# Weight loads in fewer, larger transfers behind one key tile, and query tails turned back behind them

## The chip, the core and the metric

The kernel runs on one core of a Trainium2 chip. The metric is device time in microseconds (us), lower is better. Engines are named as in the profile: PE (matrix products), PEld (its weight loads), DVE (vector), ACT (scalar and activation functions), POOL (GpSimd), SP (sync, which here only issues transfers).

## What is computed

For x of 2048 tokens by 640 features, all in bfloat16, with a token's gate g:

```python
g = sigmoid((x * gate_w).sum(-1, keepdims=True))

# a: linear attention, 32 heads of 20
q, k, v = split(x @ wqkv)
pq, pk = phi(q), phi(k)            # phi(t) = (t + 1 if t > 0 else exp(t)) + 1e-6
kv  = einsum("shd,she->hde", pk, v);  z = pk.sum(over tokens)
a   = (pq @ kv) / (pq . z + 1e-6) @ wo

# b: a mixer block and an MLP
h   = gelu(layernorm(x) @ w1)      # 640 -> 640
hs  = four groups of 160 features of h, shifted by +1, -1, +2, -2 tokens, @ w2
x1  = x + hs
b   = x1 + gelu(layernorm(x1) @ w3) @ w4     # 640 -> 1728 -> 640

out = g * a + (1 - g) * b
```

## The kernel before

Everything stays in SBUF. Tokens are cut into 16 tiles of 128 and 4 chunks of 512, features into 5 blocks of 128. "Turning" a tile means a transposing transfer, issued by SP, which puts features on the partitions.

**First stage, to 52.8 us on PE.** For each token tile PE makes 512 columns of q (`q_tile`, L900) and the keys (`k_tile`, L798); ACT's Exp and two DVE instructions make phi of them (`phi`, L788). The last 128 columns of q are made for a whole chunk at once, already turned (`q_turned`, L888); the result `mT` has to be turned back into token order by a transfer on SP (`q_back`, L896). There are four such tails. The turned x (`xT`) comes from transfers on SP (`x_turn`, L689). An event `k_done[t]` marks the last DVE instruction of key tile t.

**Second stage, 52.8 to 76 us.** PE forms GT, the product of x and phi(k) over all tokens (`gt_step`, L827); one block of it is copied by ACT to Mt and turned by SP into GT (L825). From GT and `wv` follow the heads' kv (`kvt_group`, L993), and from these and `wo` the matrix M (`m_last`, `m_first`, L1047 and L1052), stored in `M_sb`. Within this stage the layer norm of x is prepared: POOL computes the statistics of a chunk (`ln_chunk_stats`, L840) and normalises a tile into one of three `xn` slots (`normalize`, L865), SP turns it into `xnT` (`t_xn`, L871).

**Then** come w1 (`w1_group`, L1090, one block j of output features for one chunk), w2 (`w2_tile`, L1098), w3 and w4 with M's product mixed in, and the output.

**The mixer's feature order.** w1's 640 columns are used as four groups of 160, each with a shift of its own. Blocks j = 0 to 3 are the first 128 columns of each group, block 4 the four remainders of 32. Before, this order is made by the transfers: w1 is loaded by 8 transfers (128 and 32 columns of each group), w2 by 8 (128 and 32 rows of each).

**What sets the order.** Each piece of work is an item in one of several streams with dependences and a model of time (`_Items.run`, L336): among the items whose dependences have been emitted, a planner takes the one that can begin soonest, and so writes out a fixed instruction list for each engine. `sch.dma(queue, ...)` (L260) issues a transfer from the named engine's queue; `deps` are events that the issuing engine waits for. Each engine runs its list strictly in order, so a waiting instruction holds all behind it. The weights w1, w2, wv and wo are loaded from POOL's queue by `load_w1`, `load_w2` and `load_wvo` (L722 to L749), behind key tiles 7, 9 and 11. SP's list in this stretch is: turns of x, three query tails, GT, turns of xn. The items that place these are L955 to L979.

Of the kernel before, what the change touches and what calls it, by code (L numbers as in the profile page):

```python
# [5 lines left out]
BF16 = mybir.dt.bfloat16  # L6
# [5 lines left out]
D = 640  # L12
# [3 lines left out]
NT = S // 128  # L16
NCH = S // 512
KD = D // 128
# [398 lines left out]
def _build(nc, A_x, A_wqkv, A_wo, B_w1, B_w2, B_w3, B_w4, gate_w, out, dbg=None, stop=None):  # L417
    sch = _Sched(nc)
# [37 lines left out]
    pa = Arena(SB_LO, SB_HI - SHARED)  # L456
# [3 lines left out]
    ps = nc.alloc_psum_tensor("ps", [128, 8, 512], F32)  # L460
# [14 lines left out]
    w1 = pa.alloc("w1", [128, KD, D], BF16)  # L475
    w2 = pa.alloc("w2", [128, KD, D], BF16)
    wo_aug = pa.alloc("wo_aug", [128, 6, D], BF16)
    x_tok = pa.alloc("x_tok", [128, NT, D], BF16)
    xnT = pa.alloc("xnT", [128, KD, S], BF16)
# [3 lines left out]
    Lt = pa.alloc("Lt", [128, 6, 64], BF16)  # L483
    Mt = pa.alloc("Mt", [128, D], BF16)
    M_sb = pa.alloc("M_sb", [128, KD, D], BF16)
    zb = pa.alloc("zb", [128, D], BF16)
    dnr = pa.alloc("dnr", [128, 2, 4, H], F32)
    zc = pa.alloc("zc", [128, KD], F32)
# [13 lines left out]
    wv = wvf[:, 0:KD * D].rearrange("p (k d) -> p k d", d=D)  # L502
# [58 lines left out]
    def nfree(ap):  # L561
        n = 1
        for d_ in ap.shape[1:]:
            n *= d_
        return n
# [23 lines left out]
    def pe(fn, reads, writes, cost=500.0):  # L589
        for w_ in writes:  # L590
            sp_, rl = sch.rects(w_)
            if sp_ == "ps":
                for (_p0, _p1, lo, hi) in rl:
                    for b in range(lo // PS_BANK, (hi - 1) // PS_BANK + 1):
                        bank_pend.discard(b)
        return sch.op("pe", fn, reads, writes, cost=cost)

    def mm_group(out_ap, pairs, reads_extra=()):
        n = len(pairs)

        def fn(e, out_ap=out_ap, pairs=pairs, n=n):
            ins = None
            for i, (l, r) in enumerate(pairs):
                ins = e.matmul(out_ap, l, r, start=(i == 0), stop=(i == n - 1))  # L604
            return ins
        reads = [a for p in pairs for a in p] + list(reads_extra)
        return pe(fn, reads, [out_ap], cost=n * (max(nfree(pairs[0][1]), 24) * 0.4167 + 2.5))
# [54 lines left out]
    def memset(engf, ap, val):  # L662
        return engf(lambda e: e.memset(ap, val), [], [ap])

    def copy(engf, out_ap, in_ap):
        cost = None
        if engf is dve and in_ap.dtype == BF16 and out_ap.dtype == BF16:
            cost = 65.0 + nfree(out_ap) / 1.92
        return engf(lambda e: e.tensor_copy(out_ap, in_ap), [in_ap], [out_ap], cost=cost)
# [50 lines left out]
    k_done = {}  # L720

    def load_w1():  # L722
        dp = [k_done[7]]
        for g_ in range(4):
            sch.dma("pool", w1[:, :, 128 * g_:128 * (g_ + 1)],
                    B_w1[:, 160 * g_:160 * g_ + 128].rearrange("(k p) f -> p k f", p=128), "w1", group_total=8, deps=dp)
            sch.dma("pool", w1[:, :, 512 + 32 * g_:512 + 32 * (g_ + 1)],
                    B_w1[:, 160 * g_ + 128:160 * (g_ + 1)].rearrange("(k p) f -> p k f", p=128), "w1", group_total=8, deps=dp)

    def load_w2():  # L730
        dp = [k_done[9]]
        for g_ in range(4):
            sch.dma("pool", w2[:, g_, :], B_w2[160 * g_:160 * g_ + 128, :], "w2", group_total=8, deps=dp)
            sch.dma("pool", w2[32 * g_:32 * (g_ + 1), 4, :], B_w2[160 * g_ + 128:160 * (g_ + 1), :], "w2", group_total=8, deps=dp)

    def wo_rows(h, e, ns):
        v = A_wo[0:600, :].rearrange("(q p) d -> p q d", p=B3)
        q0 = 2 * h + e
        return v[:, q0:q0 + 4 * (ns - 1) + 1:4, :]

    def load_wvo():
        dp = [k_done[11]]
        sch.dma("pool", wv[:, :, :], A_wqkv[:, 2 * D:3 * D].rearrange("(k p) f -> p k f", p=128), "wv", deps=dp)
        for h in range(2):
            for e in range(2):
                ns = 3 - h
                sch.dma("pool", wo_aug[64 * h:64 * h + B3, e:e + 2 * ns - 1:2, :],
                        wo_rows(h, e, ns), "wo", group_total=5, deps=dp)
        sch.dma("pool", wo_aug[64:104, 4, :], A_wo[600:D, :], "wo", group_total=5, deps=dp)  # L749

    memset(pool, ones_c[:], 1.0)
    memset(pool, wkg[:, :, D:D + 1], 1.0)
# [20 lines left out]
    IT = _Items()  # L773
# [24 lines left out]
    def k_tile(t):  # L798
        tok = slice(128 * t, 128 * (t + 1))
        b = pair()  # L800
        mm_group(ps[:, b, 0:512], [(xT[:, k, tok], wkg[:, k, 0:512]) for k in range(KD)])
        mm_group(ps[:, b + 1, 0:130], [(xT[:, k, tok], wkg[:, k, 512:D + 2]) for k in range(KD)])
        k_out(t, b)
# [61 lines left out]
    def normalize(which, t, st):  # L865
        sx = slot("xn", 3)
        tag_set("xn", sx, (which, t))
        xn_slots[(which, t)] = sx
        ts(pool, xn[:, sx, :], x_tok[:, t, :], st[:, 6, t:t + 1], st[:, 7, t:t + 1], ALU.mult, ALU.add)
# [18 lines left out]
    def q_turned(c):  # L888
        b = bank()
        sl = qx_slot[c] = slot("tl", 4)  # L890
        mm_group(ps[:, b, :], [(wq[:, k, 512:D], xT[:, k, 512 * c:512 * (c + 1)]) for k in range(KD)])
        phi(b, mT[:, sl, :], n=512)
# [3 lines left out]
    def q_back(c):  # L896
        sl = qx_slot[c]
        sch.dma("sp", pq_tok[:, 4 * c + 1:4 * c + 5, 512:D], mT[:, sl, :], "trm%d" % sl, transpose=True)

    def q_tile(t):  # L900
        tok = slice(128 * t, 128 * (t + 1))
        b = bank()
        mm_group(ps[:, b, :], [(xT[:, k, tok], wq[:, k, 0:512]) for k in range(KD)])
        phi(b, pq_tok[:, t + 1, 0:512], n=512)
# [36 lines left out]
    def addA(name, dur, fn, deps=()):  # L941
        IT.add("A", name, dur, fn, deps)
# [7 lines left out]
    for i in range(3, NT + 2):  # L950
        if i < NT:
            addA(("q", i), 1.08, lambda t=i: q_tile(t))
            addA(("k", i), 1.36, lambda t=i: k_tile(t))
            if i % 4 == 3:
                addA(("qx", i // 4), 1.08, lambda c=i // 4: q_turned(c))  # L955
                IT.add("QB", ("qb", i // 4), 0.0, lambda c=i // 4: q_back(c),
                       deps=[(("qx", i // 4), 2.5), (("t1", NT - 1), 0.0) if i == NT - 1 else (("k", i + 1), 0.0)])
        if i > 3:
            for t in range(3) if i == 4 else (i - 2,):
                addA(("g0", t), 0.27, lambda t=t: gt_tail(t), deps=[(("k", max(t, 1)), 2.0)])  # L960

    IT.add("LW", ("lw1",), 0.0, load_w1, deps=[(("k", 7), 0.0)])
    IT.add("LW", ("lw2",), 0.0, load_w2, deps=[(("k", 9), 0.0)])
    IT.add("LW", ("lwv",), 0.0, load_wvo, deps=[(("k", 11), 0.0)])

    def stats1(c):
        ln_chunk_stats(st1, c, lr[:, 4 * c:4 * c + 4, 0:1].rearrange("p t o -> p (t o)"))

    for u in range(NT):
        if u % 4 == 0:  # L970
            IT.add("S1", ("s1", u // 4), 0.0, lambda u=u: stats1(u // 4), deps=[(("k", u + 3), 1.8)])
        d1 = [(("s1", u // 4), 3.0 + 0.9 * (u % 4))]
        d1.append((("k", 13), 0.0) if u == 0 else (("n1", u - 1), 0.9))
        if u == 2:
            d1.append((("k", NT - 1), 2.0))
        if u >= 3:
            d1.append((("t1", u - 3), 0.0))
        IT.add("N1", ("n1", u), 0.0, lambda u=u: normalize(1, u, st1), deps=d1)
        IT.add("T1", ("t1", u), 0.0, lambda u=u: t_xn(1, u), deps=[(("n1", u), 1.1)] + ([(("zb",), 0.0)] if u == 12 else []))  # L979
# [110 lines left out]
    def w1_group(c, j):  # L1090
        cols = slice(512 * c, 512 * (c + 1))
        b = bank()
        mm_group(ps[:, b, :], [(w1[:, k, 128 * j:128 * (j + 1)], xnT[:, k, cols]) for k in range(KD)])
        for (p0, p1, sh) in PIECES[j]:
            o0 = 2 + 512 * c + sh
            activation(hsT[p0:p1, j, o0:o0 + 512], ps[p0:p1, b, :], ACTF.Gelu_apprx_tanh)
# [209 lines left out]
    for c in range(NCH):  # L1306
        for j in range(KD):
            deps = [(("t1", u), 0.9) for u in range(4 * c, 4 * c + 4)] if j == 0 else []
# [7 lines left out]
    for t in range(NT):  # L1316
        c = t // 4
        deps = [(("w1", c, KD - 1), GEL)]
# [8 lines left out]
    for u in range(NT):  # L1327
        deps = [(("s2", u // 4), 3.2 + 0.9 * (u % 4))]
# [8 lines left out]
    for c in range(NCH):  # L1337
        for j in range(KFF):
            deps = []
# [4 lines left out]
            if j == 0:  # L1344
                deps = deps0 + [(("t2", u), 0.9) for u in range(4 * c, 4 * c + 4)]
# [12 lines left out]
    for t in range(NT):  # L1358
        deps = [(("zb",), 1.0), (("q", max(t, 2)), 2.0), (("sg", 1), 0.0)]
        deps.append((("qb", t // 4), 3.0))  # L1360
        if t < 5:
            i = 4 * t + 3
            deps.append((("w1", i // KD, i % KD), 0.0))
        else:
            i = 3 * (t - 5)
# [7 lines left out]
    for t in range(NT):  # L1373
        g = GOF[t]
        t0, t1 = GROUPS[g]
        cl = (t1 - 1) // 4
        deps = [(("qt", t), 3.0), (("w4load",), 0.0), (("m", 1), 1.0), (("mt",), 2.5)]
# [65 lines left out]
```

## Time and profile before

| | |
|---|---|
| median of 3 runs | 259.44 us (259.2 to 259.5) |
| the profiled execution | 259.2 us |
| its span, first to last instruction | 257.9 us |
| PE busy | 255.1 us, 1478 matmuls |
| mean granted PE clock | 1.000 |
| POOL busy | 90.9 us |
| software queue (POOL's transfers) | 1168 packets, 3.28 MB |
| hardware queue of SP | 54800 packets, 21.87 MB |

A row of a group or a timeline names the line of the code, the engine, the operation, and "written<-read". In a timeline the first number is the start in us from the span's start, the second the length; x16 means that sixteen neighbouring instructions are put together, and the brackets at the end say how long the engine sat idle before and which work ended that. For transfers the table of issues gives the size and the median time from issue to landing; an issue's own length is the time of the issuing engine, not of the data. The chain of work that ended last is the path that sets the end.

### The profile page before, as it was taken

What the parts mean: (1) busy time and instruction counts of PE and PEld (TensorE: products, weight loads), DVE (VectorE), ACT (ScalarE), POOL (GpSimd) and SP (SyncE); (2) the same over time, 40 slices, a digit from 0 to 9 for tenths busy, and PEclk for the clock granted to TensorE, in tenths of its full rate; (3) what the DMA queues carried; (4) which work ended last, traced back from release to release, by engine and by line L of the source; (5) the groups of instructions that cost most, each with busy time, mean ns of one, the idle gap of its engine ahead of it and who ended that gap; (6) DMA issues with size and microseconds to landing.
All of it is one profiled execution on the core that took longest, in us unless ns stands there. A gap on an engine that the chain in (4) does not pass through costs nothing.

```text
span 257.9 us, 3904 instructions
## 1 busy us (share of the span) xinstructions
PE 255.1 (99%) x1478; PEld 126.7 (49%) x1478; DVE 144.8 (56%) x289; ACT 108.9 (42%) x224; POOL 90.9 (35%) x144
## 2 busy tenths in 40 slices
PE   8999999999999999999999999999999999999996
PEld 4555555544454545555444445444444744444744
DVE  2697888899964995589999300399700033200033
ACT  1587676651366868666854331001540100253100
POOL 5020499976952162677908000123200021300000
PEclk9999999999999999999999999999999999999999
DMA  7856699956637699372628630114130022200012
GB/s 226 226 135 114 188 137 177 262 109 126 127 76 79 125 399 293 84 100 56 121 49 117 123 60 3 31 25 127 36 17 0 3 52 80 102 1 3 0 20 102
DMA packets 57650, 26.50 MB, mean 103 GB/s; under 512 B 48884, under 2 KB 56221, under 8 KB 57632
## 3 DMA queue, kind: packets, MB, share of 16 engines
q1 hardware_dynamic: 54800, 21.87, 40.2%
q0 software_dynamic: 1168, 3.28, 5.8%
q10 hardware_dynamic: 1664, 1.11, 1.4%
q8 instruction: 11, 0.18, 0.3%
q14 instruction: 7, 0.06, 0.1%
HBM read 12.04 MB, written 2.62 MB: 57 GB/s over the span
## 4 chain that ended last, share of the span: by engine, by line
PE 99%; DVE 0%; issue 0%
PE ps L604 53%; PE ps L1213 30%; PE ps L811 8%; PE ps L922 2%; PE ps L884 1%; PE ps L1240 1%; PE ps L1128 1%; PE ps L615 1%; PE ps L1009 0%; PE ps L1038 0%; PE ps L923 0%; DVE x_tok L643 0%
## 5 line engine op out<-in xcount | busy, mean ns | idle before, releaser
L604 PE MATMUL ps<-xnT,w 128*128 128x512 bf16 x360 | 81.3, 379 | 0.0
L643 DVE SCALAR_TENSOR_TENSOR x_tok<-ps,stg,abx 128x512 bf16<-128x512 f32 (+2 forms) x17 | 12.2, 718 | 81.4 <-PE ps L1213 81.3
L660 ACT ACTIVATE h2T<-ps 128x512 bf16<-128x512 f32 x52 | 30.6, 598 | 59.5 <-PE ps L604 59.5
L604 PEld LDWEIGHTS ps<-xnT,w 128*128 128x128 bf16 x360 | 34.5, 98 | 39.8 <-issue 0.5
L1213 PE MATMUL ps<-w,h2T 128*128 128x512 bf16 (+2 forms) x221 | 45.4, 366 | 0.0
L626 POOL TENSOR_SCALAR xn<-x_tok,st 128x640 bf16<-128x640 bf16 x32 | 36.0, 1130 | 25.4 <-DMA xnT<-xn 24.9
L626 POOL TENSOR_SCALAR abx<-x_tok,stg 128x640 f32<-128x640 bf16 x16 | 15.3, 965 | 70.7 <-DVE x_tok L643 70.7
L1213 PEld LDWEIGHTS ps<-w,h2T 128*128 128x128 bf16 x221 | 21.2, 98 | 23.5
L660 ACT ACTIVATE Er<-ps 128x512 bf16<-128x512 f32 (+1 forms) x36 | 23.0, 649 | 14.6 <-PE ps L604 10.3
L659 ACT ACTIVATE junk<-x_tok 128x640 bf16<-128x640 bf16 x32 | 23.6, 738 | 3.9 <-DVE x_tok L641 3.7
L660 ACT ACTIVATE hsT<-ps 128x512 bf16<-128x512 f32 (+1 forms) x32 | 19.0, 594 | 12.5 <-PE ps L604 12.0
L604 PE MATMUL ps<-w,hsT 128*128 128x512 bf16 (+1 forms) x160 | 23.7, 299 | 0.0
L604 PE MATMUL ps<-wkg,xT 128*128 128x130 bf16 (+1 forms) x140 | 21.4, 299 | 0.0
L641 DVE SCALAR_TENSOR_TENSOR x_tok<-ps,x_tok 128x640 bf16<-128x640 f32 x16 | 13.1, 821 | 11.2 <-PE ps L604 10.5
L604 PEld LDWEIGHTS ps<-w,hsT 128*128 128x128 bf16 x160 | 13.3, 98 | 12.3
L1213 PE MATMUL ps<-M_sb,pqnT 128*128 128x512 bf16 (+2 forms) x85 | 18.6, 367 | 0.0
L811 PE MATMUL ps<-pk_tok,x_tok 128*128 128x512 bf16 x80 | 17.8, 379 | 0.0
L604 PEld LDWEIGHTS ps<-wkg,xT 128*128 128x128 bf16 x140 | 11.9, 97 | 11.4
L1157 DVE TENSOR_TENSOR pq_tok<-pq_tok,dnr 128x300 bf16<-128x300 bf16 (+1 forms) x48 | 16.9, 405 | 0.5
L634 DVE TENSOR_TENSOR qprod<-qprod,pk_tok 128x640 f32<-128x640 f32 x13 | 16.3, 1252 | 0.4
L626 DVE TENSOR_SCALAR Er<-Er 128x512 bf16<-128x512 bf16 (+1 forms) x36 | 12.3, 341 | 6.9 <-ACT Er L660 6.2
L604 PE MATMUL ps<-wq,xT 128*128 128x512 bf16 x65 | 16.2, 379 | 0.0
(87 smaller groups left out, 243.8 us busy)
## 6 DMA issues: line engine op xcount, KB each, us to landing
w<-in_B_w_dram SPq DMA_DIRECT2D x1, 2160.0 KB, 8.1
w<-in_B_w_dram SPq DMA_DIRECT2D x1, 2080.0 KB, 15.2
out_dram<-x_tok SPq DMA_DIRECT2D x3, 640.0 KB, 3.2
w<-in_B_w_dram POOLq DMA_DIRECT2D x8, 160.0 KB, 6.4
x_tok<-in_A_x_dram SPq DMA_DIRECT2D x6, 160.0 KB, 3.7
x_tok<-in_A_x_dram SPq DMA_DIRECT2D x1, 960.0 KB, 5.3
wv<-in_A_wqkv_dram POOLq DMA_DIRECT2D x1, 800.0 KB, 5.7
x_tok<-in_A_x_dram SPq DMA_DIRECT2D x1, 640.0 KB, 4.6
```

What stands on the lines that cost most here:

```text
L604: ins = e.matmul(out_ap, l, r, start=(i == 0), stop=(i == n - 1))
L615: ins = e.transpose(o, s_, ident[:])
L626: return engf(lambda e: e.tensor_scalar(out_ap, in_ap, s1, s2, op0, op1), rd, [out_ap], cost=cost)
L634: return engf(lambda e: e.tensor_tensor(out_ap, a, b_, op), [a, b_], [out_ap], cost=cost)
L641: return dve(lambda e: e.scalar_tensor_tensor(out_ap, in0, scalar, in1, op0, op1, accum_out=accum), rd, [out_ap, accum], cost=cost + 70.0)
L643: return dve(lambda e: e.scalar_tensor_tensor(out_ap, in0, scalar, in1, op0, op1), rd, [out_ap], cost=cost)
L659: return act(lambda e: e.activation(out_ap, in_ap, func, bias=bias, scale=scale, accum_out=accum), rd, wr, cost=cost)
L660: return act(lambda e: e.activation(out_ap, in_ap, func, bias=bias, scale=scale), rd, wr, cost=cost)
L811: ins = e.matmul(o, l, r, start=(t0 + q_ == 0), stop=(t0 + q_ == NT - 1))
L922: ins = e.matmul(ps[:, b, 0:512], l, w[:, k, 0:512], start=(k == 0), stop=(k == KD - 1))
L1157: dve(lambda e, o=o, i0=i0, i1=i1: e.tensor_tensor(o, i0, i1, ALU.mult), [i0, dnr[:, 1, sd, :]], [o], cost=cost)
L1213: ins = e.matmul(o, l, r, start=first and i == 0, stop=last and i == len(prs) - 1, skip_group_check=True)
```

## The change

- w1 is loaded as it lies in memory, by one transfer instead of eight. Blocks 0 to 3 are read from it at a stride of 160 columns; the four remainders are put together by a copy on POOL into a new buffer `w1r`, which lies where M's first block will be stored later.
- w2 is loaded by five transfers instead of eight: the four groups' first 128 rows in one.
- All of w1, w2, wo and wv are issued behind key tile 8, in this order. Before, wv went ahead of wo.
- The first three query tails are turned back behind key tiles 14, 15 and 15 instead of 4, 8 and 12.
- The normalisation of tile 1 is placed behind the last piece of GT's tail block.

```diff
     M_sb = pa.alloc("M_sb", [128, KD, D], BF16)
+    w1r = pa.alias("w1r", [128, KD, 128], BF16, pa.last_addr, KD * D * 2)
...
     def load_w1():
-        dp = [k_done[7]]
+        sch.dma("pool", w1[:, :, :], B_w1.rearrange("(k p) f -> p k f", p=128), "w1", deps=[k_done[8]])
+
+    def w1_rest():
+        copy(pool, w1r[:, :, :].rearrange("p k (g f) -> p k g f", g=4),
+             w1[:, :, :].rearrange("p k (g f) -> p k g f", g=4)[:, :, :, 128:160])
+
+    def load_w2():
+        dp = [k_done[8]]
+        rows = B_w2.rearrange("(g r) d -> r g d", r=160)
+        sch.dma("pool", w2[:, 0:4, :], rows[0:128, :, :], "w2", group_total=5, deps=dp)
         for g_ in range(4):
-            sch.dma("pool", w1[:, :, 128 * g_:128 * (g_ + 1)],
-                    B_w1[:, 160 * g_:160 * g_ + 128].rearrange("(k p) f -> p k f", p=128), "w1", group_total=8, deps=dp)
-            sch.dma("pool", w1[:, :, 512 + 32 * g_:512 + 32 * (g_ + 1)],
-                    B_w1[:, 160 * g_ + 128:160 * (g_ + 1)].rearrange("(k p) f -> p k f", p=128), "w1", group_total=8, deps=dp)
-
-    def load_w2():
-        dp = [k_done[9]]
-        for g_ in range(4):
-            sch.dma("pool", w2[:, g_, :], B_w2[160 * g_:160 * g_ + 128, :], "w2", group_total=8, deps=dp)
-            sch.dma("pool", w2[32 * g_:32 * (g_ + 1), 4, :], B_w2[160 * g_ + 128:160 * (g_ + 1), :], "w2", group_total=8, deps=dp)
+            sch.dma("pool", w2[32 * g_:32 * (g_ + 1), 4, :], B_w2[160 * g_ + 128:160 * (g_ + 1), :], "w2", group_total=5, deps=dp)
...
     def load_wvo():
-        dp = [k_done[11]]
-        sch.dma("pool", wv[:, :, :], A_wqkv[:, 2 * D:3 * D].rearrange("(k p) f -> p k f", p=128), "wv", deps=dp)
+        dp = [k_done[8]]
...
         sch.dma("pool", wo_aug[64:104, 4, :], A_wo[600:D, :], "wo", group_total=5, deps=dp)
+        sch.dma("pool", wv[:, :, :], A_wqkv[:, 2 * D:3 * D].rearrange("(k p) f -> p k f", p=128), "wv", deps=dp)
...
                 IT.add("QB", ("qb", i // 4), 0.0, lambda c=i // 4: q_back(c),
-                       deps=[(("qx", i // 4), 2.5), (("t1", NT - 1), 0.0) if i == NT - 1 else (("k", i + 1), 0.0)])
+                       deps=[(("qx", i // 4), 2.5), (("t1", NT - 1), 0.0) if i == NT - 1 else (("k", min(14 + i // 4, NT - 1)), 0.0)])
...
-    IT.add("LW", ("lw1",), 0.0, load_w1, deps=[(("k", 7), 0.0)])
-    IT.add("LW", ("lw2",), 0.0, load_w2, deps=[(("k", 9), 0.0)])
-    IT.add("LW", ("lwv",), 0.0, load_wvo, deps=[(("k", 11), 0.0)])
+    IT.add("LW", ("lw1",), 0.0, load_w1, deps=[(("k", 8), 0.0)])
+    IT.add("LW", ("lw2",), 0.0, load_w2, deps=[(("k", 8), 0.0)])
+    IT.add("LW", ("lwv",), 0.0, load_wvo, deps=[(("k", 8), 0.0)])
+    IT.add("LW", ("w1r",), 0.0, w1_rest, deps=[(("k", 10), 0.0)])
...
+        if u == 1:
+            d1.append((("g0", NT - 1), 0.0))
...
-        mm_group(ps[:, b, :], [(w1[:, k, 128 * j:128 * (j + 1)], xnT[:, k, cols]) for k in range(KD)])
+        mm_group(ps[:, b, :], [(w1[:, k, 160 * j:160 * j + 128] if j < 4 else w1r[:, k, :], xnT[:, k, cols]) for k in range(KD)])
```

## The prediction

> **What bounds the kernel now.** I read the busy shares and the clock row first, then PE's busy time by stage, then the chain of work that ended last, and only then the queues that the change touches (POOL, SP and the table of DMA issues).
>
> ```profile
> PE 255.1 (99%) x1478; PEld 126.7 (49%) x1478; DVE 144.8 (56%) x289; ACT 108.9 (42%) x224; POOL 90.9 (35%) x144
> PEclk9999999999999999999999999999999999999999
> ```
>
> The clock is at its top digit in all 40 slices (mean 1.000), so none is to be won there. Since a matmul's end is modelled, 99% alone proves nothing. The table by stage has, after the stretch and its length, PE's busy us, then PEld, DVE, ACT and POOL:
>
> ```profile
> 9.40:52.80 43.40, 43.40 (x270) 22.51 (x269) 35.66 (x67) 31.46 (x80) 23.65 (x45) 1.00 0.86 168
> 52.80:69.80 17.00, 17.00 (x83) 7.81 (x81) 16.44 (x18) 5.53 (x10) 13.96 (x16) 1.00 0.57 113
> 69.80:256.00 186.20, 186.12 (x1086) 92.22 (x1083) 89.28 (x195) 69.28 (x132) 49.96 (x67) 1.00 0.37 79
> ```
>
> From 9.4 us to the end PE is idle for 0.08 us. That it isn't padded is seen by the chain (start, length, what):
>
> ```profile
> 46.58 2.44 PE ps L604 x15
> ...
> 49.29 3.52 PE ps L604 x20
> 52.81 17.00 PE ps L811 x81
> 69.82 4.32 PE ps L604 x20
> ```
>
> Twenty matmuls of 512 columns take 4.32 us, 0.216 each. The 81 of GT are 78 of 512 columns and 3 of 128; a pair of one each takes 0.27 in the chain, so 128 columns cost 0.055: 78 x 0.216 + 3 x 0.055 = 17.01, and 17.00 is measured. There is no hidden wait at the two places where the change could remove one: before 69.82, when the first w1 group needs turned rows 0 to 3, w1 and its weights, and in the k and q stage before it. **PE is the bound and has nothing to wait less for.**
>
> **What the change does to PE, ACT and DVE.** Laid side by side, their instruction streams in both programs are the same, in the same order and with the same waits by engine; only the four w1 groups of the fifth block read `w1r` instead of a tail of `w1`. No matmul is added or taken away: 0 us. The left operand lies elsewhere in SBUF; a weight load takes 98 ns beside a matmul of 216, so it could double and stay hidden. What remains is whether POOL, SP and the DMA queues make PE wait.
>
> ```profile
> 31.93 11.41 POOL L285 DMA_DIRECT2D w<-in_B_w_dram  x16
> 46.28 0.95 POOL L285 DMA_DIRECT2D wv<-in_A_wqkv_dram  x1
> 47.24 3.29 POOL L285 DMA_DIRECT2D wo_aug<-in_A_wo_dram  x5
> 50.58 0.88 POOL L626 TENSOR_SCALAR xn<-x_tok,st 128x640 bf16<-128x640 bf16 x1
> 29.07 8.30 SPq L281 DMA_TRANSPOSE xT<-x_tok  x6
> 37.41 6.68 SPq L281 DMA_TRANSPOSE pq_tok<-mT  x3
> 56.77 1.20 SPq L281 DMA_TRANSPOSE GT<-Mt  x1
> 58.02 13.46 SPq L281 DMA_TRANSPOSE xnT<-xn  x10
> ```
>
> **POOL.** Now: 11.41 + 0.95 + 3.29 = 15.65 us of issuing, 31.93 to 50.58 with one chunk of statistics (43.38 to 46.28, 2.90 us) between. After: the start moves from key tile 7 to key tile 8, whose last DVE instruction ends at 33.93. Then w1 in one transfer (0.95, the row of wv, which has the same shape), w2's 128 rows in one (from 0.87, the usual step between w1's issues now, to 0.95), four of 32 rows (the second half of the 16 takes 4.29 us for 8, so 0.54 each, 2.15), wo 3.29, wv 0.95: 8.3 us, to 42.2. The copy into `w1r` is not in the trace: at the low end it goes as the small POOL rows (0.30 for 128x60), at the high end twice the slowest pass over 128x640 (1.78), 3.6; I take the median row of such a pass, 0.93, as it has the same size. It waits for w1, and behind it on POOL stand the statistics of chunk 2, the normalisation of tile 0 and all later ones. w1 lands at the soonest 5.7 us after its issue (wv's row), so 39.6; at the latest when all 3.28 MB of the software queue are through. These at 209 GB/s (the mean from 50 to 56 us, nearly all loads) take 15.7 us, from about 36, so 51.7. By the first, statistics run from 43.1 to 46.0 and tile 0 is normalised at 46.9 instead of 51.46; by the second the copy ends at 52.6 and tile 0 is done at 56.4. **Neither reaches PE:** the first w1 group is at 69.82, and tiles 1 to 3 follow the statistics of chunk 3, which ACT holds back to 52.63 now anyway.
>
> **SP.** The turning of tile 0 moves ahead of three turned query tails and of GT: it goes out at about 47 instead of 58.02. The tails go from 37.41 to about 48, 1.3 us each (the row without back-pressure), done issuing by 52; GT waits for ACT's Mt until 56.74 as now. Tiles 1, 2 and 3 now go out at 59.34, 60.66 and 61.98 and land 2.7 later; with one turn less ahead each goes 0 to 1.3 earlier. Now tile 3 is in at 64.7, so the first group has 5.1 us of slack, afterwards 5.1 to 6.4. Tile 7 (67.43 + 2.7 = 70.1, needed at 77.36) has 7.2. If loads and tails delay all of it by the worst landing of any xnT turn (8.0 instead of 2.7), 5.3 is gone and 0.2 would be left to pay. The tails themselves are first read by DVE at 82.8; from 52 they have 30 us.
>
> **The other side of the transfers.** The loads that used to trickle out over 11.4 us now stand in the queues within 8.3 us, beside turns of x that the q and k tiles read.
>
> ```profile
> wv<-in_A_wqkv_dram POOLq DMA_DIRECT2D x1, 800.0 KB, 5.7
> w<-in_B_w_dram POOLq DMA_DIRECT2D x8, 160.0 KB, 6.4
> pq_tok<-mT SPq DMA_TRANSPOSE x4, 7.6
> ```
>
> The turns of x tiles 10 to 15 go out at 29.07, 30.31, 31.63, 32.95, 34.2 and 36.1; the first lands in 2.6, the last two in 7.1 and 7.2 us, because the loads run beside them. So tile 14 is in at 41.3, needed at 46.58, and tile 15 at 43.3, needed at 49.29: slack 5.3 and 6.0. Afterwards the loads start 2 us later, which spares tiles 12 and 13, and 14 and 15 meet a fuller queue. At best each lands in 2.6; at worst no turn moves until all loads are through at 51.7, tile 14 comes at 53.0 and PE pays 6.4. I take the row nearest to it, turns beside loads, 7 to 9 us (8.9 is the slowest tail): 36.1 + 8.9 = 45.0, in time. Cost 0, with 6.4 kept for the range.
>
> The packets counted over the queues are 2.8 KB on the software queue (3.28 MB in 1168) and 0.4 KB on the turning one. The Trainium skill, "DMA: Bandwidth & Descriptors", section "Queues, rings and completion order", speaks against the change here: an engine takes turns between queues by whole packets, so larger load packets make each turn wait longer; this case's 2.6 against 7.2 agrees in direction, no row shows larger packets. By it the sum would gain a stall of 0 to about 3 us; by the landings of this trace it gains none.
>
> DVE's pass over Er (128x640) takes 0.33 us at 28.64 and 40.58, but 0.64 at 32.44, when POOL starts issuing. A k tile needs DVE for 0.33 + 0.82 + 0.29 + 0.69 = 2.13 of PE's 2.71 us, so 0.3 more still fits. The bound is 0 to 0.3 on each of about four tiles, 1.2 in all; there were four such slow passes before at no PE idle time, so I take 0. The Trainium skill, "SBUF — State Buffer", section "SBUF: two separate sides", holds that POOL's descriptor writing and such DVE passes lock each other out; by it POOL's 8.3 us would stretch, into slack.
>
> **The sum.** 0 + 0 + 0 against the profiled execution's own 259.2 (span 257.9 and 1.3 around it). The median of the three runs is 259.44, 0.24 above it; a run like those gives **259.4**.
>
> **The rivals.**
> - **The burst holds up the turning of x, and it is slower.** Place: queries 14 and 15 at 46.58 and 49.29. It decides once a turn lands more than 12.4 us after issue for tile 14 or 13.2 for tile 15. For it: landings already go from 2.6 to 7.2, and the burst is denser. Against it: 5 us of slack. Price 0 to 6.4, middle 3: 262.4. Chance 0.08.
> - **POOL's new wait holds the first w1 group.** After the copy come 2.9 (statistics), 0.9, 3.9 (chunk 3), three tiles of 1.47 and 3.0 for issue and landing, 15.1 in all, so it decides when the copy ends after 54.7, w1 landing 20 us after issue where wv took 5.7. Price, at 2 us past that: 261.4. Chance 0.03.
> - **DVE is slowed past its slack** while POOL issues: tenths on some tiles, 260.2. Chance 0.04.
> - **The change doesn't do what it says:** the larger transfers land no sooner. All are needed late (w1 69.82, w2 80.6, wv 76.29, wo 92.9), so 259.4 as well. Chance 0.10.
> - **Faster.** Only the first 9.4 us hold idle time or slow spots, and nothing there is changed; a chance difference of some tenths, 258.7. Chance 0.05.
>
> **How the numbers follow.** The forecast, loads earlier and PE unmoved, has 0.70. A measurement of this kernel tells 0.2%, 0.52 us, from no change: 258.9 to 259.9 is "same", with 0.70 + 0.10 = 0.80; slower has 0.08 + 0.03 + 0.04 = 0.15, faster 0.05. The range reaches from 258.9 over the DVE case and the small end of the first rival to 260.5; what lies above (large stalls, 0.09) and below (0.05) is left out.
>
> **What would show it.** Right: PE's chain without gaps, its span within 0.5 us of 257.9; POOL done issuing near 42, not 50.6; tile 0 turned near 47; the three tails after it. Wrong: an idle entry of PE behind a DMA on xT (k and q stage) or xnT (69.82), the turns of tiles 14 and 15 landing in over 12 us, or the copy into `w1r` after 54.

## The result, and the profile after

The changed kernel takes **269.37 us** (median of 6 runs, 265.74 to 271.02) against 259.47 (6 runs, 259.20 to 260.23): ratio 1.0306, 95% interval 1.0250 to 1.0363. It is slower by 3%; the prediction said no change, 258.9 to 260.5. The profiled execution took 270.29, its span is 269.0. The ratio is over the three runs that lie within 1.5% of the fastest (265.74, 268.34, 268.47); the other three count as slow and the profiled one is among them, so the pieces below add up to 11.1 us where the ratio stands for some 8.

Busy shares and the clock row of the changed kernel's page:

```profile
PE 257.3 (96%) x1478; PEld 127.1 (47%) x1478; DVE 143.3 (53%) x289; ACT 108.9 (40%) x224; POOL 85.1 (32%) x135
PEclk9999999858999999999999999999999999999999
```

PE's work is the same 1478 matmuls. What is new is a dip of the clock in slices 8 to 10 (6.7 us each, so some 47 to 67 us), where it was 9 everywhere, and a PE share of 96% instead of 99%. The list of what PE waited for (total us, times, longest):

```profile
PE ps L605 <- DMA xT<-x_tok: 8.3, 1, 8.3
PE ps L885 <- PEq L1432: 0.8, 1, 0.8
PE ps L923 <- DMA wq<-in_A_wqkv_dram: 0.5, 2, 0.4
```

The first line is new: one wait of 8.3 us for a turn of x. The 0.8 stands in every profile of this kernel, the 0.5 on the first loads comes and goes (0.4 to 1.1 in four of the experiments, with nothing changed there). The chain of waits between 44 and 82 us (start, length, what):

```profile
36.40 21.54 DMA xT<-x_tok
57.94 0.05 issue
57.99 5.88 PE ps L605 x20
63.87 17.00 PE ps L812 x81
```

The turn of x tile 15 goes out at 36.40 and lands at 57.94. Then the 20 matmuls of that tile (query, key, turned queries) take 5.88 us where they took 3.52, and GT's 81 take 17.00, as before, but begin at 63.87 instead of 52.81. So 11.06 us are lost up to here: 8.3 of waiting, 5.88 - 3.52 = 2.36 of slow matmuls, and about 0.4 already before the wait (PE comes to it at 49.7, where query 15 began at 49.29 before). Span against span is 269.0 - 257.9 = 11.1, so nothing is lost after it. The clock, by stretches (the last three columns are granted clock, DMA share and GB/s):

```profile
46.00:50.00 4.00, 3.70 (x26) 1.89 (x24) 3.58 (x6) 2.51 (x7) 0.73 (x1) 1.00 1.01 136
50.00:54.00 4.00, 0.00 (x0) 0.00 (x0) 1.15 (x2) 0.95 (x4) 0.00 (x0) 0.78 1.29 201
54.00:58.00 4.00, 0.01 (x1) 0.02 (x2) 0.00 (x0) 0.00 (x0) 0.00 (x0) 0.50 0.81 125
58.00:62.00 4.00, 4.00 (x10) 1.48 (x11) 0.98 (x2) 0.60 (x1) 0.00 (x0) 0.50 0.40 80
62.00:64.00 2.00, 2.00 (x15) 1.06 (x13) 0.40 (x2) 1.17 (x3) 0.27 (x1) 0.88 0.00 0
64.00:66.00 2.00, 2.00 (x13) 0.94 (x12) 1.89 (x5) 0.83 (x4) 1.37 (x4) 1.00 0.03 8
```

PE stops at 49.7; the clock is at half all the way from 54 until 62, four us after PE has work again at 57.99, and full from 64. The 0.78 from 50 to 54 is 1.76 us at 0.50 and the rest at 1.00, so it fell near 52.2, some 2.5 us after PE stopped. Ten matmuls fit into 58 to 62, at 0.216 us it would be 18.

Now the landings. In a window of some hundredths of a us around one issue, the issue table holds that issue alone (last number: us from issue to landing). Tiles 14 and 15 in the changed kernel, then the same two in the kernel before:

```profile
xT<-x_tok SPq DMA_TRANSPOSE x1, 10.2
xT<-x_tok SPq DMA_TRANSPOSE x1, 21.5
```

```profile
xT<-x_tok SPq DMA_TRANSPOSE x1, 7.1
xT<-x_tok SPq DMA_TRANSPOSE x1, 7.2
```

Tile 14 (issued 35.08) lands at 45.3, still ahead of its query at some 46.8. Tile 15 is three times as late as before. POOL, the queue it meets:

```profile
34.34 3.88 POOL L285 DMA_DIRECT2D w<-in_B_w_dram  x6 [2.03 <-DVE pk_tok L644]
38.21 3.25 POOL L285 DMA_DIRECT2D wo_aug<-in_A_wo_dram  x5
41.44 0.92 POOL L285 DMA_DIRECT2D wv<-in_A_wqkv_dram  x1
42.36 0.74 POOL L670 COPY w1r<-w 128x640 bf16<-128x640 bf16 x1
```

All 12 loads go out in one row, 34.34 to 42.36; in the kernel before, 22 took from 31.93 to 50.58. In the issue table `wv` lands 16.5 us after 41.44:

```profile
wv<-in_A_wqkv_dram POOLq DMA_DIRECT2D x1, 800.0 KB, 16.5
```

That is 57.94, the moment at which tile 15 lands. From these two numbers came the theory that the experiments test: **a turn of x that stands beside a POOL queue which doesn't run empty comes through only as the loads do.** The rivals: the larger packets alone hold it up; the gate alone does (all loads from key tile 8); the tails moved behind the turns do, or their absence ahead; and for the 2.36, that the slow matmuls have another cause than a clock that fell while PE idled.

### The profile page after: what moved, and what is told of

Its sections match the earlier page's. It is cut to its first block, busy times and chain, and to the rows that moved or that the text cites. A ratio compares the mean times of both kernels' runs of the same rounds, so it can differ in the third digit from the quotient of the medians.

```text
span 269.0 us, 3894 instructions
## 1 busy us (share of the span) xinstructions
PE 257.3 (96%) x1478; PEld 127.1 (47%) x1478; DVE 143.3 (53%) x289; ACT 108.9 (40%) x224; POOL 85.1 (32%) x135
## 3 DMA queue, kind: packets, MB, share of 16 engines
q0 software_dynamic: 912, 3.28, 6.0%
## 4 chain that ended last, share of the span: by engine, by line
PE 78%; DMA 15%; SPq 6%; issue 0%; DVE 0%
PE ps L605 39%; PE ps L1217 29%; DMA xT<-x_tok 8%; DMA x_tok<-in_A_x_dram 7%; PE ps L812 7%; SPq L281 5%; PE ps L1244 1%; PE ps L1132 1%; SPq L285 1%; PE ps L1013 0%; PE ps L1042 0%; DVE x_tok L644 0%
## 5 line engine op out<-in xcount | busy, mean ns | idle before, releaser
L605 PE MATMUL ps<-xnT,w 128*128 128x512 bf16 x340 | 76.7, 379 | 0.0
L605 PEld LDWEIGHTS ps<-xnT,w 128*128 128x128 bf16 x340 | 32.7, 98 | 38.0 <-issue 0.5
L627 POOL TENSOR_SCALAR xn<-x_tok,st 128x640 bf16<-128x640 bf16 x32 | 37.2, 1172 | 24.0 <-DMA xnT<-xn 23.5
L627 POOL TENSOR_SCALAR abx<-x_tok,stg 128x640 f32<-128x640 bf16 x16 | 15.3, 966 | 70.7 <-DVE x_tok L644 70.7
L661 ACT ACTIVATE Er<-ps 128x512 bf16<-128x512 f32 (+1 forms) x36 | 23.0, 648 | 25.6 <-PE ps L605 20.9
L1217 PEld LDWEIGHTS ps<-w,h2T 128*128 128x128 bf16 x221 | 21.1, 98 | 23.6
L660 ACT ACTIVATE junk<-x_tok 128x640 bf16<-128x640 bf16 x32 | 23.6, 738 | 3.9 <-DVE x_tok L642 3.7
L605 PE MATMUL ps<-wq,xT 128*128 128x512 bf16 x65 | 17.2, 398 | 8.3 <-DMA xT<-x_tok 8.3
L605 PE MATMUL ps<-wkg,xT 128*128 128x130 bf16 (+1 forms) x140 | 22.5, 309 | 0.0
L627 DVE TENSOR_SCALAR Er<-Er 128x512 bf16<-128x512 bf16 (+1 forms) x36 | 11.6, 322 | 18.0 <-ACT Er L661 17.1
L605 PEld LDWEIGHTS ps<-w,hsT 128*128 128x128 bf16 x160 | 13.3, 98 | 12.3
L642 DVE SCALAR_TENSOR_TENSOR x_tok<-ps,x_tok 128x640 bf16<-128x640 f32 x16 | 13.2, 822 | 11.1 <-PE ps L605 10.4
L605 PEld LDWEIGHTS ps<-wkg,xT 128*128 128x128 bf16 x140 | 12.4, 101 | 12.5 <-issue 1.9
## 6 DMA issues: line engine op xcount, KB each, us to landing
wv<-in_A_wqkv_dram POOLq DMA_DIRECT2D x1, 800.0 KB, 16.5
```

Of the source, the lines that this page charges most:

```text
L627: return engf(lambda e: e.tensor_scalar(out_ap, in_ap, s1, s2, op0, op1), rd, [out_ap], cost=cost)
L642: return dve(lambda e: e.scalar_tensor_tensor(out_ap, in0, scalar, in1, op0, op1, accum_out=accum), rd, [out_ap, accum], cost=cost + 70.0)
L660: return act(lambda e: e.activation(out_ap, in_ap, func, bias=bias, scale=scale, accum_out=accum), rd, wr, cost=cost)
L661: return act(lambda e: e.activation(out_ap, in_ap, func, bias=bias, scale=scale), rd, wr, cost=cost)
L1217: ins = e.matmul(o, l, r, start=first and i == 0, stop=last and i == len(prs) - 1, skip_group_check=True)
```

## The experiments

**Each part of the change by itself.** Three kernels start from the kernel before, or come to the same: only the gates, only the transfers (with the copy into `w1r`, and the normalisation of tile 1 behind GT's last tail piece, kept), only the late tails.

e3_gates_only, on the kernel before (in this and the next ones the items in the stream of loads, `lw1`, `lw2` and `lwv`, get the same key tile as the wait):

```diff
     def load_w1():
-        dp = [k_done[7]]
+        dp = [k_done[8]]
...
     def load_w2():
-        dp = [k_done[9]]
+        dp = [k_done[8]]
...
     def load_wvo():
-        dp = [k_done[11]]
+        dp = [k_done[8]]
```

> The kernel before with only the gates changed: all 22 small loads are issued behind key tile 8, tails early. POOL needs 15.7 us to issue them, so its queue runs empty between issues. T and P: the turns of tiles 14 and 15 go through in the gaps as before, landing in 7 to 9 us, no stall, 259.4 to 260. If the gate alone were the cause (all loads asked for at once), 262 to 269.

e4_large_only, on the changed kernel:

```diff
-        sch.dma("pool", w1[:, :, :], B_w1.rearrange("(k p) f -> p k f", p=128), "w1", deps=[k_done[8]])
+        sch.dma("pool", w1[:, :, :], B_w1.rearrange("(k p) f -> p k f", p=128), "w1", deps=[k_done[7]])
...
     def load_w2():
-        dp = [k_done[8]]
+        dp = [k_done[9]]
...
     def load_wvo():
-        dp = [k_done[8]]
+        dp = [k_done[11]]
...
-                       deps=[(("qx", i // 4), 2.5), (("t1", NT - 1), 0.0) if i == NT - 1 else (("k", min(14 + i // 4, NT - 1)), 0.0)])
+                       deps=[(("qx", i // 4), 2.5), (("t1", NT - 1), 0.0) if i == NT - 1 else (("k", i + 1), 0.0)])
```

> The kernel before with only the transfers changed: w1 in one transfer (with the copy on POOL), w2 in five, wo ahead of wv, each behind its old gate (7, 9, 11), tails early. T: less stands in the queue at a time, tile 14 and 15 land later than before (8 to 14 us), stall 0 to 3, 259.4 to 262. P: the large packets alone do it, stall near 8, 266 to 270.

f2_tails_late_only, on the kernel before:

```diff
-                       deps=[(("qx", i // 4), 2.5), (("t1", NT - 1), 0.0) if i == NT - 1 else (("k", i + 1), 0.0)])
+                       deps=[(("qx", i // 4), 2.5), (("t1", NT - 1), 0.0) if i == NT - 1 else (("k", min(14 + i // 4, NT - 1)), 0.0)])
...
+        if u == 1:
+            d1.append((("g0", NT - 1), 0.0))
```

> The kernel before with one part of the change alone: the three turned query tails go back behind key tiles 14 and 15, and the turning of tile 0 waits for GT's last tail tile; transfers and gates as before. By the theory (POOL's queue must never run empty for a turn to be held up) this is 259.2 to 259.8, and the turns of tiles 14 and 15 land in at most 8 us. If the tails that now stand closely behind the turns of x at SP delay them, PE waits for a turn and the time is above 260.5.

(The last two lines of the edit hold back the normalisation of tile 1, as in the change, not the turning of tile 0.)

Measured: gates only 259.63 us, ratio 1.0000 (0.9963 to 1.0037); transfers only 259.55, 0.9988 (0.9961 to 1.0016); late tails only 259.36, 0.9990 (0.9972 to 1.0007). **No part alone costs more than the 0.4% that these intervals leave.** The turns of tiles 14 and 15 land after 5.8 and 9.9 us, 6.9 and 8.7, 6.2 and 8.4. So larger transfers are not the cause by themselves, nor is the gate: with small transfers POOL still needs some 16 us to issue them, with three gates it pauses between.

Small transfers do not keep the queue empty, though. In e3 the three tails that SP turns behind tile 15 land after 10.7, 12.3 and 14.0 us; this is the third:

```profile
pq_tok<-mT SPq DMA_TRANSPOSE x1, 14.0
```

The loads issued from 45.95 on land there 13.8 to 15.3 us after their issue, so by then they stand in the queue too. The turns of tiles 14 and 15 go out in the row's first 2 us, behind one and two loads of 160 KB. The tails are needed late, so their delay costs nothing.

**The gate of wv and wo back to key tile 11.** e1_wvo_at_11, on the changed kernel:

```diff
     def load_wvo():
-        dp = [k_done[8]]
+        dp = [k_done[11]]
```

> The changed kernel with one gate put back: wv and wo are issued behind key tile 11 again, w1 and w2 stay behind tile 8 in few large transfers. Theory T (backlog): while POOL's queue holds bytes, a turn of x gets one small packet for each load packet, so a turn lands about when the backlog ends; in the changed kernel tile 15's turn, issued at 36.4, landed at 57.9 together with wv. With 1.6 MB less standing in the queue until about 42, tile 15 comes earlier; expected 260 to 264, a stall of 0 to 4 us in place of 8.3. Theory P (packet size alone: each load packet is larger, whatever stands behind it): the stall stays near 8, 268 to 270.

260.32 us, ratio 0.9993 (0.9955 to 1.0031; one of ten runs took 264.87); in the profile PE waits for no turn. There w1 and w2 go out from 33.90 to 37.79, and the next load at 43.86. Tile 15, issued at 36.54 beside them, lands in

```profile
xT<-x_tok SPq DMA_TRANSPOSE x1, 10.0
```

at 46.5, with 3 us to spare. The whole loss goes when the row of loads is broken once; the large transfers and the late tails stay.

**Early tails with the row of loads.** e2_tails_early puts `("k", i + 1)` back in the changed kernel and leaves all else.

```diff
-                       deps=[(("qx", i // 4), 2.5), (("t1", NT - 1), 0.0) if i == NT - 1 else (("k", min(14 + i // 4, NT - 1)), 0.0)])
+                       deps=[(("qx", i // 4), 2.5), (("t1", NT - 1), 0.0) if i == NT - 1 else (("k", i + 1), 0.0)])
```

> The changed kernel with the three query tails turned back early again, behind key tiles 4, 8 and 12. They stand behind tile 15's turn on SP, so theories T and P expect no change of the stall: 268 to 270. If the order of the tails were the cause (theory Q), the time would go back to 259 to 261.

272.6 us (267.24 to 275.59; the runs spread too far for a ratio); PE waits for the turn of x 11.8 us in three pieces, the longest 10.2. Tiles 14 and 15 land after 22.3 and 20.9 us. The late tails neither cause the loss nor prevent it.

**The same loads in one row, where no turn of x is.** e8_all_at_11 gates all of them behind key tile 11, f3_all_at_9 in the same three places and items behind key tile 9. For e8:

```diff
-        sch.dma("pool", w1[:, :, :], B_w1.rearrange("(k p) f -> p k f", p=128), "w1", deps=[k_done[8]])
+        sch.dma("pool", w1[:, :, :], B_w1.rearrange("(k p) f -> p k f", p=128), "w1", deps=[k_done[11]])
...
     def load_w2():
-        dp = [k_done[8]]
+        dp = [k_done[11]]
...
     def load_wvo():
-        dp = [k_done[8]]
+        dp = [k_done[11]]
```

> The changed kernel with all loads still in one go and large, but behind key tile 11 (about 42), when all turns of x have landed. T: no turn of x beside the loads, each lands in 2.6 to 2.9, no stall, 259.2 to 259.8; the loads end near 58 and the first normalised tiles are turned beside their end, still ahead of 69.8. If the burst itself costs PE time wherever it stands (say through POOL's or DVE's delay), 262 or more.

> After, with all loads behind key tile 9 instead of 8, 2.7 us later; the turn of tile 14 then goes out about when the first transfer does, that of tile 15 one after it. If a turn is held up only by loads that stand ahead of it or beside it in the queue, tile 15 is still issued beside them and can land as late as the last load: a stall of 0 to 9 us, time 259.4 to 270. If only the turn that meets a queue already 1 us or more full is held up, tile 14 lands in 3 to 6 us, tile 15 in under 13 and the time is 259.3 to 260.5. The landing of tile 15 against that of the last load tells which: equal to it within 0.5 us by the theory that a turn lands when the queue empties, long before it by the other.

e8: 260.03 us, ratio 0.9990 (0.9957 to 1.0023). f3: 260.17 us, ratio 1.0009 (0.9989 to 1.0029; one of ten runs took 264.01). The last turn of x lands in 2.9 us in e8 and 3.3 in f3. In f3 tile 15 went out at 35.55, 1.3 us ahead of POOL's first load at 36.85, so it did not meet the queue, and what that run was to tell (a turn within the first us of the loads) it tells by another turn: a query tail, issued alone at 37.47, 0.6 us behind the first load.

```profile
pq_tok<-mT SPq DMA_TRANSPOSE x1, 7.8
```

One turn, alone beside a full queue, needs 7.8 us, not the 15 until the queue is empty. And POOL in f3, with `wv`'s row of the issue table:

```profile
36.85 3.89 POOL L285 DMA_DIRECT2D w<-in_B_w_dram  x6 [4.73 <-DVE pk_tok L644]
40.73 3.26 POOL L285 DMA_DIRECT2D wo_aug<-in_A_wo_dram  x5
43.98 0.92 POOL L285 DMA_DIRECT2D wv<-in_A_wqkv_dram  x1
```

```profile
wv<-in_A_wqkv_dram POOLq DMA_DIRECT2D x1, 800.0 KB, 8.5
```

The loads begin 2.5 us later than in the changed kernel and are through at 43.98 + 8.5 = 52.5 instead of 57.94. The same 3.28 MB take 15.6 us (210 GB/s) here, 16.1 (204) in e8, and 34.34 to 57.94, 23.6 us (139 GB/s), in the changed kernel. **Turns and loads slow each other.** The changed kernel's queues show it (packets, MB, share of 16 engines' time), first from 46 to 56 us, then from 56 to 58, when the loads run out:

```profile
q0 software_dynamic: 388, 1.49, 79.4%
q1 hardware_dynamic: 558, 0.13, 26.5%
```

```profile
q1 hardware_dynamic: 709, 0.17, 85.4%
q0 software_dynamic: 18, 0.05, 6.5%
```

Beside 388 packets of loads (q0), 558 of turns (q1) begin in ten us; beside the last 18, 709 in two.

**Fewer bytes in the row.** e5_wv_at_13 takes `wv` out (0.82 of 3.28 MB), e6_wo_at_13 takes `wo` out in its place; each goes behind key tile 13. For e6 (e5 is the same with the two exchanged):

```diff
-    def load_wvo():
-        dp = [k_done[8]]
+    def load_wv():
+        sch.dma("pool", wv[:, :, :], A_wqkv[:, 2 * D:3 * D].rearrange("(k p) f -> p k f", p=128), "wv", deps=[k_done[8]])
+
+    def load_wo():
+        dp = [k_done[13]]
...
-        sch.dma("pool", wv[:, :, :], A_wqkv[:, 2 * D:3 * D].rearrange("(k p) f -> p k f", p=128), "wv", deps=dp)
...
-    IT.add("LW", ("lwv",), 0.0, load_wvo, deps=[(("k", 8), 0.0)])
+    IT.add("LW", ("lwv",), 0.0, load_wv, deps=[(("k", 8), 0.0)])
     IT.add("LW", ("w1r",), 0.0, w1_rest, deps=[(("k", 10), 0.0)])
+    IT.add("LW", ("lwo",), 0.0, load_wo, deps=[(("k", 13), 0.0)])
```

> The changed kernel with wv alone issued later, behind key tile 13 (about 48); w1, w2 and wo stay behind tile 8. The backlog beside tile 15's turn is 2.5 MB in place of 3.3. Theory T (the bytes standing in POOL's queue decide): between the 10.0 us that 1.6 MB gave and the 21.5 that 3.3 MB gave, so tile 15 lands 13 to 17 us after its issue, a stall of 0 to 4: 260 to 263. If wo is the culprit (its rows of 60 and 40 partitions): 20 us or more, 267 to 270. If wv is: 10 us, 259.5.

> The mirror of it: wo behind key tile 13, wv behind tile 8 right after w2. Again 2.5 MB beside the turn. T: the same as with wv late, 260 to 263, tile 15 landing in 13 to 17 us. If wv's one large transfer is the culprit: 20 us or more, 267 to 270. If wo is: 10 us, 259.5.

e5: 271.94 us, ratio 1.0472 (1.0423 to 1.0522; the ratio is rough, as the kernel before ran from 259.06 to 269.68 beside it). e6: 268.83 us, 261.66 to 270.95, too wide for a ratio. I had expected too little: three quarters of the bytes cost as much in all four runs of e5 and in three of four of e6. PE's first wait in e5 (query 13) and its last in e6 (query 14), with start, busy time, what, and the idle time before it in brackets, each followed by the landing of tile 15:

```profile
48.70 2.31 PE L605 MATMUL ps<-wq,xT 128*128 128x512 bf16 x5 [4.45 <-DMA xT<-x_tok]
```

```profile
xT<-x_tok SPq DMA_TRANSPOSE x1, 18.8
```

```profile
55.43 2.32 PE L605 MATMUL ps<-wq,xT 128*128 128x512 bf16 x5 [6.29 <-DMA xT<-x_tok]
```

```profile
xT<-x_tok SPq DMA_TRANSPOSE x1, 17.5
```

In e5 that is 56.6, the last transfer of `wo` lands at 56.4; in e6 55.8, `wv` at 55.5. Both profiles have three turns of x beside the loads (tiles 13 to 15) instead of two, as POOL's start and SP's turns stand up to about a us differently to each other from run to run: in the changed kernel's profile the loads begin 0.8 us after tile 13's turn, in these two 0.3 and 0.4 ahead of it. That may be the second quantity that decides, along with the bytes: how many turns are in the queue when the row of loads begins. It is read from these profiles; no run varies it by itself.

**The clock.** e7_filler puts 30 spare matmuls ahead of query 15, f1_filler_both 20 ahead of query 14 and 20 ahead of query 15 (their results are read by nobody), so that PE doesn't idle. For f1 (e7 has `i == NT - 1` and 30):

```diff
+            if i >= NT - 2:
+                addA(("fill", i), 0.0, lambda: warmup(512 * 20, 0.0))
             addA(("q", i), 1.08, lambda t=i: q_tile(t))
```

> The changed kernel with 30 matmuls on constants (6.5 us, results not used) put on PE ahead of query 15, where PE waits for the turn. They add work but keep PE from standing idle. If the slower q and k work after the wait (5.88 us in place of 3.52) is the clock's, lowered because PE stood idle, then the clock stays at 1.00, that work takes 3.5 us again and the time falls by about 2 us, to 266 to 268. If it is not the clock's doing, the time stays at 268 to 270; if the wait for the turn is shorter than I think, it rises by up to 6.5.

> After, with 20 spare matmuls of 512 columns (4.32 us at full clock, their results are read by nobody) ahead of query 14 and 20 more ahead of query 15, so that PE works while it waits for the turn of x tile 15. If the 2.36 us by which queries, keys and turned queries of tile 15 were slower in the changed kernel come from the clock that falls while PE idles, they take 3.52 us again at a granted clock near 1.0, the stall proper is mostly filled, and the time comes out at 266.5 to 268.5, less than the changed kernel with 8.64 us more work in it. If those matmuls are slow for another reason (they read data that has just landed, or lie beside the loads), they still take near 5.9 us and the time is 269 to 272.

e7: 276.3 us, ratio 1.0602 (1.0509 to 1.0694). It missed its target: in its profile tiles 13 and 14 were late too, PE's waits (1.93 and 5.46 us) stood ahead of queries 13 and 14, and the 6.5 us of spare matmuls came on top. f1: ratio 1.0368 (1.0309 to 1.0427), its runs at 267.97 (the profiled one), 269.56, 270.77 and 277.25; only the profiled one is within what I expected. There PE waits for no turn at all, and the 20 matmuls of tile 15 have the clock and length

```profile
57.90:61.42 3.52, 3.47 (x20) 1.75 (x20) 1.13 (x3) 1.48 (x4) 0.03 (x1) 1.00 0.00 0
```

3.52 us at 1.00, against 5.88 at 0.62 in the changed kernel. That span is 266.7 = 257.9 + 8.64 of spare matmuls + 0.2, so with PE kept busy nothing else is lost. In f1 these matmuls run after the transfers (DMA share 0.00) and 6.9 us after their data landed, so f1 alone leaves the rival that fresh data or transfers beside them slow them. A row of e6 speaks against it: query 13 begins right after its turn landed, beside the loads and after a short wait, and its five matmuls take the usual time (2.32 in the changed kernel):

```profile
46.26 1.25 PE L605 MATMUL ps<-wq,xT 128*128 128x512 bf16 x5 [1.40 <-DMA xT<-x_tok]
```

So 2.36 us of the loss are the clock, which falls in the wait. By the timed runs alone it would not be seen, since the landings vary by more. They do so here: tile 15 landed after 15.7 us, at 51.05, and `wv` at 41.09 + 15.1 = 56.2.

That takes the first form of my theory down: a turn beside the loads does **not** have to wait until the queue is empty. In the changed kernel, e5 and e6 the last turn landed within half a us of the last load, in f1 5 us ahead of it, and f3's lone tail 7 us ahead.

**What fits all of them.** In the changed kernel's window from 34 to 58 us the two queues moved

```profile
q0 software_dynamic: 880, 3.28, 67.5%
q1 hardware_dynamic: 3252, 0.79, 34.7%
```

(packets, MB, share of 16 engines' time). That is 3.7 KB and 0.30 us a packet for the loads (67.5% of 24 us x 16 engines over 880) and 0.24 KB for the turns. A turn of 128x640 (164 KB) is then 674 packets, 42 on each engine, the loads are 55. If an engine gives one load packet ahead of each turn packet, a turn needs, as an estimate, about 42 x 0.295 = 12.4 us while loads stand there, and a second one behind it as much again: 10.2 for tile 14, and from its landing at 45.3 another 12.6 to tile 15's. A tail of 128x512 has 34 packets, at f3's 0.23 us (73.8% of the 17 us from 36 to 53, x 16, over 880 packets) some 7.8 us; 7.8 was measured. The Trainium skill, "DMA: Bandwidth & Descriptors", section "Queues, rings and completion order", says that an engine takes turns between the queues by whole packets; these landings agree with it in direction. The counts bear it out one for one only for f3's tail: 484 load packets begin between its issue and its landing, 30 on an engine, for its 34. For tiles 14 and 15 it is too simple: 438 begin from 35.08 to 45.30 and 442 from there to 57.94, 27 and 28 on an engine, where one for one asks for 42 each time, and all loads together have only 55. So the agreement of 12.4 with 12.6 is in part chance; what is shown is that here the second turn lands as the loads run out. How the engines share their time stays open. No run has the same bytes in smaller packets at the same pace, because POOL takes 0.54 to 0.87 us for each small transfer it issues; so whether packet size or only the full queue counts isn't separated.

## Why the prediction was wrong

- **PE is the bound and has nothing to wait less for:** right. Every piece of PE's chain after tile 15 has the length that it had, within 0.01 us.
- **The step that failed** is "I take the row nearest to it, turns beside loads, 7 to 9 us (8.9 is the slowest tail): 36.1 + 8.9 = 45.0, in time. Cost 0". It measured 21.5: 36.40 + 21.5 = 57.9, 8.3 us behind PE. The row came from a queue that POOL filled at the pace of its issuing, 22 transfers in 15.65 us with a pause. The change took just that pace away, and with it what the row rested on. I counted the bytes and the moment of the loads, but not how many packets of a turn stand beside how many of the loads. The trace before would have allowed a rough estimate: from 31.9 to 52 us its turning queue has 0.24 KB a packet, so 42 of a turn on each engine, and a load packet takes 0.20 us there (58.6% of 20.1 us x 16 over 931), 8.5 us for one turn beside a full queue and 17 for two in a row, over the 13.2 that I had given as the point of decision. It holds for a full queue alone, which that kernel did not have beside tile 15 (7.2 us), and it takes one load packet for each turn packet, which the counts above bear out in part. The sentence on the skill's rule in the prediction, "0 to about 3 us", was too small for the same reason: it counted no packets.
- **The upper end, 51.7 us for the loads and 6.4 for PE,** was no upper end: it let the loads run at 209 GB/s, as they do with hardly a turn beside them (204 and 210 in e8 and f3). Beside the turns they ran at 139, and were through at 57.94. The clock was not in the price at all: 2.36 us. And the range ended at 260.5, so it left out even the 6.4.
- **The rival "the burst holds up the turning of x"** had the mechanism, the place (query 15; query 14 was spared by 1.5 us, and in the profiles of e2, e5, e6 and e7 queries 13 and 14 were held) and the point of decision (10.2 under 12.4, 21.5 over 13.2). Its price, 0 to 6.4, was 10.7, and its chance of 0.08 was too small: "5 us of slack" was set against a delay for which the trace before has no row.
- **POOL:** right. Issuing took 8.02 us and was done at 42.36 (42.2), the copy 0.74 (0.93), tile 0 normalised at 46.73 (46.9).
- **SP:** tile 0's turn goes out at 46.76, as worked out, but lands only 11.7 later, and the three tails behind it took 9.77 us to issue, not 4:

```profile
46.76 1.20 SPq L281 DMA_TRANSPOSE xnT<-xn  x1
48.00 9.77 SPq L281 DMA_TRANSPOSE pq_tok<-mT  x3
```

  None of it reaches PE, as the slack was there. They stand beside the same row of loads as tile 15's turn.
- **DVE slowed by POOL's issuing:** no cost seen; no wait of PE on DVE.
- **Larger transfers land no sooner:** mixed. w1 is in 6.8 us after its issue, wv 16.5 after its own instead of 5.7, at 57.94 instead of 52.0. Nobody needs them before 69.82, so it brought nothing either way.

## What to carry to other kernels

A landing time is a property of what else is in the queues, not of the transfer: before bunching loads into one row, see which other transfers go out in those microseconds, and take a landing measured beside slowly issued loads as a lower bound. Slow issuing can be what protects the latency of the transfers that the bound engine waits for, as long as these go out early in it (in e3 the later ones took up to 14.0 us); breaking the row once (e1), or starting it once the last urgent transfer is out (f3 by 1.3 us, e8 by 6.9), costs nothing and keeps the large transfers. Where PE is bound, price a stall of several us with the clock that it loses on top.

## What the runs showed of the hardware

- Turns and loads beside each other cost throughput. The stretch with all loads in it, in the changed kernel and in f3 (last columns: clock, DMA share, GB/s):

```profile
34.00:58.00 24.00, 15.71 (x101) 8.06 (x100) 14.29 (x27) 11.98 (x31) 11.91 (x21) 0.88 1.03 171
```

```profile
36.00:53.00 17.00, 16.89 (x104) 8.81 (x105) 14.21 (x26) 12.06 (x32) 12.11 (x22) 1.00 1.03 233
```

  The DMA engines are equally busy, and move 171 GB/s against 233.
- The clock fell to 0.50 in the waits of 6.29 us (e6's last, ahead of 55.43) and 8.3, and stayed at 1.00 after 1.40 (e6's first, ahead of 46.26). In the changed kernel it was full again some 4.5 us after PE had work (0.88 from 62 to 64 is half a us at 0.50, the rest at 1.00). The two stretches of e6:

```profile
46.00:48.00 2.00, 1.75 (x9) 0.80 (x10) 0.54 (x1) 0.56 (x3) 1.43 (x4) 1.00 1.23 198
...
54.00:56.00 2.00, 0.57 (x2) 0.28 (x3) 0.00 (x0) 0.00 (x0) 0.47 (x1) 0.50 1.24 163
```

  The Trainium skill, "TensorE: Matmul & The Clock Gate", section "HAM oscillation — how this bites in real kernels", puts the limit at idle gaps of about 3.4 us. These rows lie on either side of it, but e5 shows a shorter gap that is enough. Its second wait is 3.06 us, 4.4 us of work after the one before it; the clock falls within it (0.82 from 54 to 56), and the five matmuls behind it take 2.32 us instead of 1.25:

```profile
54.00:56.00 2.00, 0.00 (x0) 0.00 (x0) 0.81 (x1) 0.37 (x2) 0.89 (x1) 0.82 1.28 77
...
56.19 2.32 PE L605 MATMUL ps<-wq,xT 128*128 128x512 bf16 x5 [3.06 <-DMA xT<-x_tok]
```

  So in this case 1.93 us (e7's first wait, five matmuls in 1.25 behind it) kept the clock and 3.06 lost it.
- The same program's landings vary: 265.74 to 271.02 us for the changed kernel, where the kernel before keeps within 1.1 us in the six runs beside it. It does not always: in the experiments' sessions single runs of it took up to 269.68, and in four of them the granted clock was 0.987 to 0.994 instead of 1.000, as when PE stalls; no trace shows what it waited for there. In the profiles, a few tenths between POOL's first load and SP's turns decide whether two or three turns meet the row.
